# Attention with projected keys, then a gated feed-forward: an earlier projection, another tile for two sums, and two reorderings

## The chip, the cores and the metric

The kernel runs on one NeuronCore of one Trainium2 chip. The metric is the device time of one execution in microseconds. A core has five engines with an instruction queue each: TensorE (PE, matrix products into the eight PSUM banks), VectorE (DVE), ScalarE (ACT), GpSimd (POOL) and SyncE (SP). Each works its own queue in order and waits on semaphores for the others. Here GpSimd issues the loads from DRAM that also convert to bf16, and SyncE issues stores, transposing DMAs and small transfers. All DMAs run on the same 16 DMA engines.

## The reference

Inputs are q, k, v of shape (8 batches, 8 heads, 1024 positions, 64), the projections E and F (64 x 1024) and the weights w_in (512 x 2048) and w_out (2048 x 512), all float32.

```
k_proj = einsum('ks,bhsd->bhkd', E, k)
v_proj = einsum('ks,bhsd->bhkd', F, v)
attn   = softmax(q @ k_proj^T / 8)            # over the 64 projected positions
x      = attn @ v_proj, heads side by side    # (8192, 512)
h      = x @ w_in
g      = h / (1 + exp(-1.702 * h))
out    = g @ w_out                            # (8192, 512)
```

## The kernel before

**Tiling.** The 8192 tokens are cut into 16 blocks of 512 tokens; a batch is two blocks, so block j belongs to batch j // 2, and block 6 is the first of batch 3. For each batch the kernel loads k, v and q (`load`, `load_kv`, `load_q`), projects k and v over the sequence (`proj`: 32 matmuls into one PSUM bank), casts the projected k into `k_b`, transposes it by DMA into `kt`, casts the projected v into `vq`, and transposes q by DMA into `qT`. For each block it then computes the scores and their exponentials, the sums over the 64 projected positions, their reciprocals spread to all partitions by a trip through DRAM, the values times the reciprocals (giving `xT`), and the two products of the feed-forward.

**Feed-forward.** From block 1 (second product) and block 2 on, both products use a fast scheme: a two by two split of each product into seven products of sums instead of eight. The first product's seven are `P1` to `P7` of a unit `u0` to `u3`; they need the sums `xw` of x (`xs`, line 499) and the sums `late` of w_in. The second product's are `F1` to `F7`, each in two halves `.0` and `.1` of eight matmuls; they need the sums `sg` of g (`gs` and `g_sum`, line 507) and `tw` of w_out. The copies and additions between them are the `c`, `d` and `Fc`, `Fd`, `Fo` steps on VectorE and ScalarE. A next product adds onto a bank only once the copy of its earlier state is made.

**Order.** Blocks 0 and 1, and the first product of block 2, are issued by loops over slots: `at(j, slot, f)` puts `f` into block j's slot, and `filled` runs it there. Six sums of w_in (`w_in_sums`, lines 486 and 490) are put into slots 4, 6, 8, 10, 12 and 14 of block 2; the sums of g of that block follow slots 7, 13 and 15, ahead of what is in the slot. From then on, order is written out by hand: `STEPS` is a list of words for one block period, with a suffix such as `+1` for a step of the next block, and `AHEAD` is a list of steps of other blocks that are done at a given point of the first period, where there is no earlier period to have done them. `pj@6:7` in it means step `pj` for block 6 with its PSUM bank given as 7. A step's instructions go to the queues of several engines at once, so its place in the list is its place in each of these queues.

**Steps of the change.** `su` makes the sums of the exponentials of a block on TensorE (line 719), `den` copies them from PSUM to SBUF on VectorE (line 723), `ga` gathers them by DMA to a small tile (line 322), `rc` takes the reciprocals (line 727), `sr` writes them to DRAM (line 731) and `sb` spreads them into `rbc` by two DMAs (line 735). `mv` multiplies the values by `rbc` (line 713). `pj`, `kb`, `kd`, `vq` project a batch, cast and transpose (lines 183, 620, 748). `hold` copies one element of `kt` on GpSimd (line 740), so that what follows in GpSimd's queue waits until the transpose has landed. `ld` loads k and v of the next batch (line 58), `qd` transposes q (line 263) and then loads the next batch's q (line 70).

In the period from block 2 to block 3, the kernel before does `pj kb kd vq hold ld qd` of block 6 at the end, after `u0.g21` of block 3, and `rc sr sb` of block 4 after `F4.1` of block 2. The tile for `den` has one buffer:

```
            if j not in rdens:
                rdens[j] = att.tile([P, 2, TB], F32, name="den", bufs=1)
            nc.vector.tensor_copy(rdens[j][:, t, :], live[f"D{t}"])
```

In block 15, the last, the F words of `STEPS` run functions from `ffn2_parts`. A table `more` puts half 2.1 next to 7.0, so that the halves run as 1.0 1.1 2.0 6.0 6.1 2.1 7.0 5.0 5.1 7.1 4.0 4.1 3.0 3.1. There `7.1` is followed by an addition on VectorE (line 575), and 4.0 adds onto the bank that this addition reads.

Of the kernel before, what the change touches and what calls it, by code (L numbers as in the profile page):

```python
# [9 lines left out]
F32 = mybir.dt.float32  # L10
# [7 lines left out]
def kernel(ctx, tc, q, k, v, E, F,  # L18
# [5 lines left out]
    P = 128  # L24
# [5 lines left out]
    TB = 512  # L30
# [7 lines left out]
    att = ctx.enter_context(tc.tile_pool(name="att", bufs=2))  # L38
    work = ctx.enter_context(tc.tile_pool(name="work", bufs=2))
# [135 lines left out]
    kvps, qT, expT, xT, rbc, rdens = {}, {}, {}, {}, {}, {}  # L175
# [91 lines left out]
    def eight(outs, lhsTs, rhss, w=32):  # L267


        for i, ro in ((0, (LO, HI)), (1, (HI, LO))):  # L270
            for c in range(0, KP, w):
                for ri, r in zip((LO, HI), ro):
                    nc.tensor.matmul(outs[i][r.start + c:r.start + c + w], lhsTs[i][ri, c:c + w], rhss[i][ri],  # L273
                                     start=True, stop=True)
# [20 lines left out]
    def gelu_table():  # L295
        nc.scalar.preload_act_table(AF.Gelu_apprx_sigmoid)

    def x_of(h):
        if h not in xT:
            xT[h] = att.tile([P, KC, TB], BF16, name="xT")  # L300
        return xT[h]
# [192 lines left out]
    def x_sum(j, i):  # L494

        x = xT[j]
        x11, x12, x21, x22 = x[:, KLO, TLO], x[:, KLO, THI], x[:, KHI, TLO], x[:, KHI, THI]
        in0, in1 = ((x12, x11), (x22, xw[:, 0]), (x22, x12), (x21, xw[:, 1]))[i]
        nc.vector.tensor_tensor(xw[:, i], in0, in1, op=ALU.subtract)

    def g_sum(j, i, c0, n):

        lo, hi = slice(c0, c0 + n), slice(FH + c0, FH + c0 + n)
        g, t = gT, [sg[:, i, c0:c0 + n] for i in range(4)]
        in0, in1 = ((g[:, lo, THI], g[:, hi, THI]), (t[0], g[:, lo, TLO]), (g[:, lo, TLO], g[:, lo, THI]),
                    (g[:, hi, TLO], t[1]))[i - 1]
        nc.vector.tensor_tensor(t[i - 1], in0, in1, op=ALU.add if i == 1 else ALU.subtract)  # L507

    def ffn2_ops(j):
        g = gts[j]  # L510
        return {1: (g[:, FLO, TLO], b11), 2: (g[:, FHI, TLO], b21), 3: (sg[:, 3], b22),
                4: (g[:, FHI, THI], tw[:, 3]), 5: (sg[:, 0], tw[:, 0]), 6: (sg[:, 1], tw[:, 1]),
                7: (sg[:, 2], tw[:, 2])}
# [90 lines left out]
    def step(name, j, banks=None):  # L604
# [7 lines left out]
        i, t = p[0], int(p[-1]) if p[-1].isdigit() else p[-1]  # L612
        b, c = divmod(j, NB2)

        def new(n, shape):
            live[n] = bank(banks.pop(0) if banks else BANK[n], shape)
            return live[n]
# [12 lines left out]
        if i[0] == "F" and i[1:].isdigit():  # L630
            i = int(i[1:])
            n = ("FD", "FB", "FG")[OF[i]]
            if i in (1, 5) and t == 0:
                new(n, [P, 2, MH])
            x, w = ffn2_ops(j)[i]
# [21 lines left out]
        elif i[0] == "u":  # L657
            n, m = int(i[1]), int(i[1]) % 2
# [3 lines left out]
            u1, u2 = uu[0][:, m], uu[0][:, 2 + m]  # L662
            lo, hi = slice(2 * n, 2 * n + 2), slice(FH + 2 * n, FH + 2 * n + 2)
            if t[0] == "P":
                i = int(t[1])
                x = xT[j]
# [7 lines left out]
                for r in range(2):  # L674
                    for c in range(KC // 2):
                        f = (2 * n + r) * P
# [17 lines left out]
        elif i[:2] == "gs":  # L694
            g_sum(j, int(i[2]), 4 * t, 4)
        elif i == "xs":
            x_sum(j, t)
        elif i == "sc":
            if j not in expT:
                expT[j] = att.tile([P, HP, TB], BF16, name="expT", bufs=3)  # L700
            eight([new(f"S{t}{e}", [P, TB]) for e in range(2)], [kts[b % 2][:, 2 * t + e, :] for e in range(2)],
                  [qT[b][:, c * JB:(c + 1) * JB, 2 * t + e, :] for e in range(2)])
        elif i == "ex":
            u = int(p[1])
            nc.scalar.activation(expT[j][:, 2 * u + t, :], live[f"S{u}{t}"], AF.Exp, scale=scale)
        elif i == "gt":
            gelu_table()
        elif i == "va":
            eight([new(f"V{t}{e}", [P, TB]) for e in range(2)], [vqs[b % 2][:, 2 * t + e, :] for e in range(2)],
                  [expT[j][:, 2 * t + e, :] for e in range(2)])  # L710
        elif i == "mv":
            u = 2 * int(p[1]) + t
            nc.vector.tensor_tensor(x_of(j)[:, u, :], live[f"V{p[1]}{t}"], rbc[j][:, u, :], op=ALU.mult)  # L713
        elif i == "su":
            d_ps = [new(f"D{e}", [P, TB]) for e in range(2)]
            for q_ in range(HP):
                for e in range(2):
                    r = HI if (q_ + e) % 2 else LO
                    nc.tensor.matmul(d_ps[e][32 * q_:32 * q_ + 32], ones[r, :32], expT[j][r, q_, :], start=True, stop=True)
        elif i == "den":  # L720
            if j not in rdens:
                rdens[j] = att.tile([P, 2, TB], F32, name="den", bufs=1)
            nc.vector.tensor_copy(rdens[j][:, t, :], live[f"D{t}"])  # L723
        elif i == "ga":
            gather(j)()
        elif i == "rc":
            nc.vector.reciprocal(rdens[j], rdens[j])
        elif i == "sr":
            n = rdens[j].shape[1]
            rdr[j] = dram.tile([HP, 2, TB], F32, name="rdr")  # L730
            nc.sync.dma_start(out=rdr[j].rearrange("p e (r n) -> (p e r) n", n=n), in_=rdens.pop(j))
        elif i == "sb":
            rbc[j] = att.tile([P, HP, TB], F32, name="rbc", bufs=1)
            for e, r in enumerate((LO, HI)):
                nc.sync.dma_start(out=rbc[j][r], in_=rdr[j][None, :, e, :].to_broadcast([D, HP, TB]))
        elif i == "pj":
            kvps[b] = new("PJ", [P, H, D])
            proj(b)()
        elif i == "hold":
            nc.gpsimd.tensor_copy(held, kts[b % 2][:1, 0, :1])  # L740
        elif i == "ld" and b + 1 < B:
            load_kv(k, kt, b + 1, "k_sb")
            load_kv(v, vt, b + 1, "v_sb")
        elif i == "kb":
            tmps["kb"] = att.tile([KP, H, D], BF16, name="k_b")
            copy(tmps["kb"], kvps[b][LO])
        elif i == "kd":
            nc.sync.dma_start_transpose(out=kts[b % 2], in_=tmps["kb"].rearrange("k h d -> k (h d)"))
        elif i == "vq":
            r, xs_ = ((LO, X_LO), (HI, X_HI))[t]  # L750
            copy(vqs[b % 2][r].rearrange("k (u e) d -> k u e d", e=2),
                 kvps[b][HI].rearrange("k (u x) d -> k u x d", x=4)[:, :, xs_, :])
        elif i == "qd":
            q_dma(b)()
            if b + 1 < B:
                load_q(b + 1)
        elif i != "ld":
            raise KeyError(name)
# [14 lines left out]
    def at(j, slot, *fs):  # L773
        fill.setdefault((j, slot), []).extend(fs)
# [60 lines left out]
    at(2, 3, spread(3, nc.gpsimd), lambda: load(3))  # L835
    at(2, 1, proj(2), kv_out(2, nc.scalar.copy))
    for i, f in enumerate(w_in_sums()):
        at(2, 4 + 2 * i, f)
    def filled(j, slot):
        for f in fill.pop((j, slot), []):  # L840
            f()
# [2 lines left out]
    for j in range(NBLK):  # L844
# [9 lines left out]
        if j == 0:  # L854
            parts = [(n, range(8 * g, 8 * g + 8)) for n in range(JB) for g in range(2)]
# [10 lines left out]
        parts = ffn2_parts(j, 5, 6, 7, None)  # L866
        for s, (i, t) in enumerate((i, t) for i in (1, 5, 6, 2, 7, 4, 3) for t in range(2)):
# [4 lines left out]
        (2, None):  # L872
            "F1.0@2 F1.1@2 Fc1@2 sc.1@4 sc.0@4 ex.1.0@4 ex.1.1@4 F2.0@2 ex.0.0@4 ex.0.1@4 F2.1@2 sc.1@5 "
            "F6.0@2 sc.0@5 F6.1@2 ex.1.0@5 ex.1.1@5 ex.0.0@5 ex.0.1@5 gt@3 Fo0@2 Fc2@2 va.0@3:6,1 va.1@3:5,7 "
            "mv.0.0@3 mv.0.1@3 mv.1.0@3 mv.1.1@3 F7.0@2 su@4:0,3 den.0@4 den.1@4 ga@4 F7.1@2 ",
        (2, "F4.1"): "rc@4 sr@4 sb@4",
        (2, "u0.g21+1"): "pj@6:7 kb@6 kd@6 vq.0@6 vq.1@6 hold@6 ld@6 qd@6",
    }

    def ahead(j, after):  # L880
        for word in AHEAD.get((j, after), "").split():
            name, n = word.split("@")
            n, _, banks = n.partition(":")
            step(name, int(n), [int(x) for x in banks.split(",")] if banks else None)
            done.add((name, int(n)))

    done = set()
    for j in range(2, NBLK):
        last = j == NBLK - 1
        parts = ffn2_parts(j, BANK["FD"], BANK["FB"], 2, 5) if last else {}  # L890
        ahead(j, None)
        for word in STEPS:
            m = word.replace("-", "+-").split("+")
            name, n = m[0], j + int(m[1] if len(m) > 1 else 0)
            if last and name[0] in "Fs" and n == j and name[:2] not in ("sc", "su", "sr", "sb"):
                if name[1:2].isdigit() and name[0] == "F":
                    i, t = int(name[1]), int(name[3])
                    more = {(2, 1): [], (7, 0): [(2, 1), (7, 0)]}
                    for x in more.get((i, t), [(i, t)]):
                        parts.pop(x)()  # L900
            elif due(name, n, j) and (name, n) not in done:
                step(name, n)
            ahead(j, word)
# [33 lines left out]
```

## Time and profile before

| what | value |
|---|---|
| median of 5 runs | 491.95 us (489.44 to 492.51) |
| the profiled execution | 488.36 us |
| its span, first to last recorded work | 486.6 us |
| mean granted TensorE clock | 0.992 of full speed |
| TensorE matmuls busy | 467.2 us (96%) |
| VectorE busy | 316.7 us (65%) |
| ScalarE busy | 322.5 us (66%) |
| GpSimd busy | 83.8 us (17%) |
| read from and written to HBM | 72.88 and 16.99 MB |

Times inside a profile are microseconds from the start of its span. In the timeline, a line gives the start, the length, the engine with the line of the kernel, the operation, what it writes and reads, how many instructions are merged in it, and in brackets the idle time before it and what ended that. "PEld" is the loading of weights into TensorE and overlaps the matmuls; "SPq" is SyncE's issue of a DMA, whose data move later. In the table of waits a line is: who waited for whom, total us, number of waits, longest. The queue called q0 carries the DMAs that GpSimd issues, q1 those of SyncE and ScalarE; a share is that of 16 engines, and where packets of two transfers overlap in an engine the sum can exceed 100%.

### The profile page before, as it was taken

The numbers are of one execution on the slowest core, as the hardware profiler recorded it, in microseconds if no ns is written. First come the engines' busy times: TensorE is split into PE (matmuls) and PEld (weight loads), VectorE is DVE, ScalarE is ACT, GpSimd is POOL, SyncE is SP. The second block draws the span as 40 slices with busy tenths as digits, with TensorE's granted clock in tenths as the row PEclk, the third lists the DMA queues.
The fourth block names the chain that finished last, engine by engine and source line by source line (L and its number), as shares of the span: only waits on it lengthen the run. The fifth ranks groups of instructions, "written<-read, shape, count | busy, mean of one in ns | idle before, by whom it ended". The sixth has DMA issues, their size and how long they took to land.

```text
span 486.6 us, 10486 instructions
## 1 busy us (share of the span) xinstructions
PE 467.2 (96%) x4323; PEld 357.9 (74%) x4331; DVE 316.7 (65%) x587; ACT 322.5 (66%) x559; POOL 83.8 (17%) x104
## 2 busy tenths in 40 slices
PE   7999989998897999999999999999999999999996
PEld 3644447555676878787888878787888878888885
DVE  4503784587566576957768576957768585958561
ACT  2665463566376686967878686967878695758461
POOL 7562161061015010501014010500000000000000
PEclk9999998999899999999999999999999999999999
DMA  9999999989099999992999379982290413502022
GB/s 166 200 189 208 221 161 165 220 174 173 4 184 224 188 191 198 214 126 91 194 243 97 102 156 207 206 118 92 41 226 6 105 69 89 162 16 88 0 88 88
DMA packets 132963, 69.19 MB, mean 142 GB/s; under 512 B 98340, under 2 KB 122420, under 8 KB 132916
## 3 DMA queue, kind: packets, MB, share of 16 engines
q0 software_dynamic: 86816, 30.43, 56.5%
q1 hardware_dynamic: 46020, 37.84, 32.0%
q8 instruction: 34, 0.56, 0.5%
q10 hardware_dynamic: 80, 0.26, 0.3%
q14 instruction: 13, 0.11, 0.1%
HBM read 72.88 MB, written 16.99 MB: 185 GB/s over the span
## 4 chain that ended last, share of the span: by engine, by line
PE 75%; DMA 16%; DVE 4%; ACT 1%; issue 1%; POOL 1%; SPq 1%; DVEq 0%; POOLq 0%; ACTq 0%
PE k_ps L677 31%; PE k_ps L637 31%; PE k_ps L533 4%; DMA q_sb<-in_q_dram 4%; PE k_ps L273 3%; PE k_ps L183 2%; DMA w_in_sb<-in_moe_w_in_dram 2%; DMA w_out_sb<-in_moe_w_out_dram 2%; DMA v_sb<-in_v_dram 2%; DMA qT<-q_sb 2%; DMA kt<-k_b 2%; PE k_ps L426 1%; DVE sg L507 1%; DVE q_even L486 1%; ACT gT L693 1%
## 5 line engine op out<-in xcount | busy, mean ns | idle before, releaser
L623 DVE TENSOR_TENSOR q_even<-k_ps,q_even 128x512 f32<-128x512 f32 x104 | 70.5, 689 | 57.4 <-PE k_ps L677 55.7
L677 PE MATMUL k_ps<-xw,late 128*128 128x256 bf16 x624 | 89.6, 273 | 2.9 <-DVE den L723 2.2
L677 PEld LDWEIGHTS <-late 128*128 128x128 bf16 x832 | 80.5, 98 | 15.7 <-issue 3.0
L637 PEld LDWEIGHTS <-sg 128*128 128x128 bf16 x832 | 81.9, 99 | 12.9 <-issue 1.8
L637 PE MATMUL k_ps<-tw,sg 128*128 128x256 bf16 x624 | 78.6, 276 | 1.1 <-DVE sg L507 0.8
L693 ACT ACTIVATE gT<-k_ps 128x512 bf16<-128x512 f32 x104 | 62.2, 600 | 25.5 <-PE k_ps L677 24.0
L677 PEld LDWEIGHTS <-w_in_sb 128*128 128x128 bf16 x624 | 58.3, 98 | 16.7 <-issue 10.4
L620 ACT COPY q_even<-k_ps 128x512 f32<-128x512 f32 x65 | 37.0, 590 | 45.5 <-PE k_ps L677 45.4
L637 PEld LDWEIGHTS <-gT 128*128 128x128 bf16 x624 | 61.0, 98 | 7.8 <-issue 0.4
L677 PE MATMUL k_ps<-xT,w_in_sb 128*128 128x256 bf16 x416 | 62.2, 273 | 0.0
L693 ACT ACTIVATE gT<-q_even 128x512 bf16<-128x512 f32 x104 | 61.5, 632 | 0.0
L70 POOL DMA_DIRECT2D q_sb<-in_q_dram x48 | 42.7, 916 | 105.8 <-DMA qT<-q_sb 73.3
L637 PE MATMUL k_ps<-w_out_sb,gT 128*128 128x256 bf16 x416 | 51.6, 273 | 0.1
L507 DVE TENSOR_TENSOR sg<-gT 128x1024 bf16<-128x1024 bf16 (+2 forms) x64 | 41.4, 648 | 3.7 <-ACT gT L693 1.9
L426 PE MATMUL k_ps<-xT,w_in_sb 128*128 128x512 bf16 (+1 forms) x195 | 42.4, 370 | 0.3
L428 ACT ACTIVATE gT<-k_ps 128x512 bf16<-128x512 f32 (+1 forms) x50 | 28.9, 580 | 17.9 <-PE k_ps L426 17.7
L426 PEld LDWEIGHTS <-w_in_sb 128*128 128x128 bf16 x200 | 19.3, 98 | 21.3 <-issue 0.8
L713 DVE TENSOR_TENSOR xT<-k_ps,rbc 128x512 bf16<-128x512 f32 x52 | 33.5, 679 | 0.4 <-issue 0.4
L677 PE MATMUL k_ps<-xT,late 128*128 128x256 bf16 x208 | 31.2, 273 | 0.5 <-ACT q_even L620 0.5
L677 PE MATMUL k_ps<-xw,w_in_sb 128*128 128x256 bf16 x208 | 31.3, 273 | 0.0
L681 ACT COPY k_ps<-k_ps 128x512 f32<-128x512 f32 x52 | 29.1, 587 | 2.8 <-PE k_ps L677 2.0
L620 DVE COPY q_even<-k_ps 128x512 f32<-128x512 f32 x39 | 25.7, 686 | 8.1 <-PE k_ps L677 8.1
(135 smaller groups left out, 563.7 us busy)
## 6 DMA issues: line engine op xcount, KB each, us to landing
out_dram<-o_sb SPq DMA_DIRECT2D x31, 512.0 KB
rbc<-rdr SPq DMA_DIRECT2D x24, 512.0 KB
k_sb<-in_k_dram POOLq DMA_DIRECT2D x7, 1024.0 KB, 11.5
v_sb<-in_v_dram POOLq DMA_DIRECT2D x7, 1024.0 KB, 15.7
q_sb<-in_q_dram POOLq DMA_DIRECT2D x48, 128.0 KB, 6.5
w_in_sb<-in_moe_w_in_dram POOLq DMA_DIRECT2D x8, 256.0 KB, 11.1
w_out_sb<-in_moe_w_out_dram POOLq DMA_DIRECT2D x4, 512.0 KB, 11.5
q_even<-in_q_dram POOLq DMA_DIRECT2D x12, 128.0 KB, 14.6
```

The costliest lines, as they stand in the source:

```text
L70: nc.gpsimd.dma_start(out=qt[b][:, j], in_=qv[:, j])
L426: nc.tensor.matmul(h_ps, w_in_sb[:, kc, fc * P:(fc + 1) * P], xT[j][:, kc, ts], start=(kc == 0), stop=(kc == KC - 1))
L428: nc.scalar.activation(gts[j][:, fc, ts], h_ps, AF.Gelu_apprx_sigmoid)
L507: nc.vector.tensor_tensor(t[i - 1], in0, in1, op=ALU.add if i == 1 else ALU.subtract)
L533: nc.tensor.matmul(dst, a[:, k, tc_ * P:(tc_ + 1) * P], w[:, k], start=(first and (one or tc_ == 0) and k == 0), stop=(final and k == FH - 1),
L620: (nc.scalar.copy if n in ON_ACT else nc.vector.tensor_copy)(out_, in_)
L623: nc.vector.tensor_tensor(out_, in0, in1, op=ALU.add)
L637: nc.tensor.matmul(live[n][:, t], x[:, c, t * P:(t + 1) * P], w[:, c], start=(i in (1, 5) and t == 0 and c == 0), stop=(i in (2, 3, 4) and ...
L677: nc.tensor.matmul(live[h][:, r], a[:, c, f:f + P], w[:, c], start=(i in (1, 5) and r == 0 and c == 0), stop=(i in (2, 3, 4) and r == 1 an ...
L681: nc.scalar.copy(new(f"B{m}", [P, 2, TH]), live[f"A{m}"])
L693: nc.scalar.activation(out_, in_, AF.Gelu_apprx_sigmoid)
L713: nc.vector.tensor_tensor(x_of(j)[:, u, :], live[f"V{p[1]}{t}"], rbc[j][:, u, :], op=ALU.mult)
```

## The change

Four edits:

1. The sums of block 4 (`den`, only for block 4) go into the tile `o1_sb` of the pool `work`, which otherwise takes half of a block's output; the sums of all other blocks keep the tile `den`.
2. The last two of the six sums of w_in move from slots 12 and 14 of block 2 to slot 15, behind all sums of g of that block.
3. In the first hand-written period, half 7.1 of block 2's second product moves from the front to after `u1.c1` of block 3; the projection of batch 3 with its casts, its transpose `kd`, `hold` and `ld` moves forward to after `gs4.0` (which is `xs.3` of block 3 in the order of this period), and uses bank 1 in place of 7; `qd` moves to after `sb` of block 4.
4. In the last block the halves run as 1.0 1.1 2.0 6.0 6.1 5.0 5.1 7.0 7.1 2.1 4.0 4.1 3.0 3.1.

The number of instructions on each engine is the same.

```diff
         elif i == "den":
             if j not in rdens:
-                rdens[j] = att.tile([P, 2, TB], F32, name="den", bufs=1)
+                pool, n = (work, "o1_sb") if j == 4 else (att, "den")
+                rdens[j] = pool.tile([P, 2, TB], F32, name=n, bufs=1)
...
     for i, f in enumerate(w_in_sums()):
-        at(2, 4 + 2 * i, f)
+        at(2, (4, 6, 8, 10, 15, 15)[i], f)
...
-            "mv.0.0@3 mv.0.1@3 mv.1.0@3 mv.1.1@3 F7.0@2 su@4:0,3 den.0@4 den.1@4 ga@4 F7.1@2 ",
-        (2, "F4.1"): "rc@4 sr@4 sb@4",
-        (2, "u0.g21+1"): "pj@6:7 kb@6 kd@6 vq.0@6 vq.1@6 hold@6 ld@6 qd@6",
+            "mv.0.0@3 mv.0.1@3 mv.1.0@3 mv.1.1@3 F7.0@2 su@4:0,3 den.0@4 den.1@4 ga@4 ",
+        (2, "u1.c1+1"): "F7.1@2",
+        (2, "gs4.0"): "pj@6:1 kb@6 kd@6 vq.0@6 vq.1@6 hold@6 ld@6",
+        (2, "F4.1"): "rc@4 sr@4 sb@4 qd@6",
...
         parts = ffn2_parts(j, BANK["FD"], BANK["FB"], 2, 5) if last else {}
+        tail = [(1, 0), (1, 1), (2, 0), (6, 0), (6, 1), (5, 0), (5, 1), (7, 0), (7, 1), (2, 1), (4, 0), (4, 1)]
...
                 if name[1:2].isdigit() and name[0] == "F":
-                    i, t = int(name[1]), int(name[3])
-                    more = {(2, 1): [], (7, 0): [(2, 1), (7, 0)]}
-                    for x in more.get((i, t), [(i, t)]):
-                        parts.pop(x)()
+                    parts.pop(tail.pop(0))()
```

## The prediction

> **What bounds the kernel now.** I read the busy shares first (TensorE 96% of a 486.6 us span; the profiled execution took 488.36 us, so 1.76 lie around the span). Only TensorE's idle time can then be won, so next came its waits over the run:
>
> ```profile
> PE k_ps L273 <- DMA qT<-q_sb: 2.7, 1, 2.7
> ...
> PE k_ps L677 <- DVE den L723: 2.2, 1, 2.2
> ...
> PE k_ps L637 <- DVE sg L507: 0.8, 1, 0.8
> PE k_ps L533 <- DVE o_sb L575: 0.8, 1, 0.8
> ```
>
> Each happens once. The first three fall between 112 and 149 us, where blocks 2 and 3 meet; the fourth is in the last block. Between 180 and 460 us TensorE waits for nothing. The table by stretches (length, TensorE busy and matmuls, ..., granted clock, DMA share, GB/s) shows what the waits hide:
>
> ```profile
> 122.00:124.00 2.00, 0.09 (x1) 0.09 (x1) 1.43 (x3) 0.00 (x0) 0.00 (x0) 1.00 0.12 7
> 124.00:126.00 2.00, 2.00 (x12) 1.47 (x12) 1.39 (x3) 0.59 (x1) 0.00 (x0) 0.56 0.05 8
> 126.00:128.00 2.00, 2.00 (x13) 1.48 (x12) 0.00 (x0) 0.04 (x1) 0.00 (x0) 0.58 0.00 0
> 128.00:130.00 2.00, 2.00 (x21) 1.79 (x19) 1.53 (x3) 1.34 (x3) 0.00 (x0) 1.00 0.01 4
> ```
>
> After the wait on den the clock is near half for 4 us: 12 matmuls in 2 us, where 20 or 21 are normal. "Busy" conceals it. The DMA engines meanwhile stand still. Then the timeline of SyncE's and GpSimd's issues, batch 3's and the next batch's:
>
> ```profile
> 134.49 1.34 SPq L735 DMA_DIRECT2D rbc<-rdr  x2
> 137.10 1.23 SPq L748 DMA_TRANSPOSE kt<-k_b  x1
> 138.64 5.45 SPq L263 DMA_TRANSPOSE qT<-q_sb  x1
> ...
> 174.95 1.23 SPq L748 DMA_TRANSPOSE kt<-k_b  x1
> ...
> 184.71 1.26 SPq L735 DMA_DIRECT2D rbc<-rdr  x2
> 186.27 11.22 SPq L263 DMA_TRANSPOSE qT<-q_sb  x1
> ```
> ```profile
> 142.57 0.18 POOL L740 COPY held<-kt 1x1 bf16<-1x1 bf16 x1 [25.46 <-DMA kt<-k_b]
> 143.06 0.87 POOL L58 DMA_DIRECT2D k_sb<-in_k_dram  x1 [0.31 <-PE k_ps L677]
> ...
> 174.76 0.87 POOL L58 DMA_DIRECT2D k_sb<-in_k_dram  x1 [9.87 <-PE k_ps L677]
> ```
>
> Block 6's scores begin at 148.97, when qT has landed: **that landing, not the work before it, places everything after it.** What arrives at 146.3 or earlier waits. Last, the DMA queues (packets, MB, share) in 184 to 188 and then 188 to 192 us:
>
> ```profile
> q0 software_dynamic: 813, 0.83, 124.3%
> q1 hardware_dynamic: 5, 0.00, 0.2%
> ```
> ```profile
> q1 hardware_dynamic: 560, 0.87, 101.7%
> q0 software_dynamic: 54, 0.04, 6.5%
> ```
>
> While k and v load (q0), the rbc transfers issued at 184.71 (q1) move nothing until about 188, when the load is through; qT comes behind them and lands at 199.9, 13.6 us after its issue.
>
> **What the Trainium skill says.** "DMA: Bandwidth & Descriptors", section "Queues, rings and completion order": each DMA engine takes turns between queue rows by packets, not bytes. The trace agrees: loads of 1 KB packets run at 204 per us alone, and beside them kt's 256 B packets got 124 to 132 per us, the loads 157 to 162 (288 to 290 us). Alone, qT's packets run at 1133 per us. "TensorE: Matmul & The Clock Gate", part 1 on the HAM clock gate: an idle window of about 3.4 us halves the clock, and the window runs freely. The trace agrees in the size (0.56); 2.2 us of idle sufficed once, 2.7 us at 146 did not.
>
> **The change, part by part.** Times are the trace's, moved.
>
> *Two sums of w_in behind those of g.* VectorE's 2.29 us subtraction (106.76) and 1.22 us cast (110.97) go behind eight sums of g. F6.0's last matmul waited 0.84 for them; its successor at 112.98 comes at 111.97. No instruction is added, and late is first read at 118.9, after 113.1. **-1.0.**
>
> *Block 4's sums in o1.* den.0@5 waited 2.82 us for the gather of block 4 to read the one den tile. Now it follows the xw sums at 118.8, ends at 120.1, and u1.P5 goes at 120.64 for 123.91: **-3.3** with the first part. o1's earlier store was issued at 92.5, and its next writer, Fd1, comes 7 us after the gather: free. F7.1, moved behind block 5's sums, fills 0.87 us there; free. With the idle gone I take F5's 16 matmuls at full clock, 1.75 us for 3.50: **-4.9** at u1.P7 (127.76 becomes 122.8). If the clock is still halved, everything below is 1.75 later.
>
> *Projection of batch 3.* k and v landed by 116.2, so no data is awaited. But it takes bank 1, which u1.g11 still reads: in the trace that activation ends at 129.04, where the next matmul started at 128.20. So about 0.9 is a new wait; then 32 matmuls, 1.85 us, from 124.15 to 126.0. Behind it k_b is cast (+1.99 to +2.67 after its start), and vq.1 ends at +3.46; u3.P1 needs the same bank after 1.31 us of other matmuls: 0.35 more. Behind the cast on VectorE stand u1.d1 and Fd1, done by 128.2, before u1.P4 and F4.0 (128.1, 128.5) lose over 0.1. F4.1 comes at 129.85 for 131.69. At its old place 2.25 us fall away, so F3.0 is at 132.1 for 136.25: **-4.1**. That is all the compute gains before the scores of block 6.
>
> *Its DMAs.* kd goes at 126.85 (projection +2.70). DMA is idle, so it lands in some 2.1 us (issued at 339.18 in quiet, its packets ended at 341.1). The 1x1 copy "held" frees GpSimd at 129.0, and k and v of batch 4 are issued at about 129.5 for 143.06. rc, sr, sb follow u0.P7 as before: sr 131.1, sb 132.65 to 134.0, qd 134.1 for 138.64. **The order is turned over: the load goes ahead of rbc and qT.** A load issued at 174.76 kept the engines to 188.4, 13.6 us; this one to 143.1 alone. rbc is 1 MB at 112 packets of 2 KB per us, 4.4 us; qT's 4096 packets take 3.6. As the engines are full throughout, qT, last in its ring and of the smallest packets, ends at 129.5 + 13.6 + 4.4 + 3.6 = 151.1; with the 0.9 from last packet to landing seen at 199 us, **152.0 for 148.83: +3.1 at block 6's scores**. This price isn't in the trace of before: from below, qT keeps its 10.2 us (144.3); from above it adds the 3 us of gaps that its packets show between 192 and 199, or the late clock of F5: 155. I take the sum because it only assumes full engines.
> rbc itself lands at about 144 (shared by packets from 136 on), where mv.0.1@4 wants it at 138.2. On VectorE u2.d2 and u2.d1 are queued behind it, and u2.P4 waits for u2.d1: TensorE idles from 140.3 to about 146, then 2.0 us of work (144.3 to 146.3 in the trace; 3.7 at half clock) still reach the scores before 152. The wait is covered by qT's; without that cover it is 1.7 us over before. Such idling should halve the clock; part of the 1.75 us of one cold spell falls after 152: half, **+0.9**. Stores of block 2 wait behind qd on SyncE, until about 150; o0 is rewritten at 157: hidden, 1 us if not.
>
> *Last block.*
>
> ```profile
> 478.51 0.69 DVE L575 TENSOR_TENSOR o_sb<-k_ps,u_sb 128x512 f32<-128x512 f32 x1 [4.55 <-ACT u_sb L556]
> ...
> 479.25 1.91 PE L533 MATMUL k_ps<-tw,gT 128*128 128x256 bf16 x16 [0.84 <-DVE o_sb L575]
> ```
>
> With 2.1 (8 matmuls, 0.87 us) between 7.1 and 4.0, the 0.84 us wait is covered: **-0.85**. The store of o0's left half goes 3 us later, 0.26 MB ahead of the last ones; at 268 GB/s at most 1 us, hidden if it moves before 481.
>
> Sum: +3.1 + 0.9 - 0.85 = +3.1 us, 491.5 against 488.36. The median of the five runs is 3.6 above the profiled execution, so on its scale 491.95 + 3.1 = 495.0.
>
> **Rivals.**
> *Faster, qT lands early* (0.15). Where rbc and qT keep their trace durations under the load, qT lands at 144.3 and TensorE, at hand from 142.2, loses little: -4.6 - 0.85 = -5.4, 486.5. It decides from a landing before 147.4. For it: every compute wait named above does vanish, and at 149 to 153 us stores of 4 KB packets had over half the engines beside the load. Against: qT's packets are 256 B.
> *Stall only moved* (0.20). qT lands at 148 to 150; all compute gains end in a longer wait there and only the last block's remains: about -1, 491.
> *Two cold spells or late F5* (0.13). qT at 154 to 155 and a halved clock behind it: +5 to +6 and +1.75, 498 to 499.
> *The sum above* (0.52): landing 150 to 154, 493 to 497.
>
> **How the numbers follow.** The 8-in-10 range runs from 487.5 (within the first rival) to 499.5 (the third). The likeliest case's own is 493 to 497. 0.5% is 2.5 us, about what a measurement here can tell from no change. Faster: the first rival, 0.15. Same: the second and a sixth of the main case, 0.28. Slower: the rest, 0.57.
>
> **What would show it.** Right: no wait of F6.0 on sg, u1.P5 without idle, clock 1.00 in 118 to 124, one new wait of near 0.9 us at the projection, k_sb issued before the second rbc and qd, q1 near zero or sharing by packets for 10 us, TensorE idle ahead of u2.P4 on rbc and at block 6's scores on qT, landing near 152; no wait on L575. Wrong: qT landing under 147, or q0 starting behind qd.

## The result: 490.58 us, and the profile after

The changed kernel takes 490.58 us (median of 44 runs, 488.72 to 492.14), the kernel before 490.11 us (79 runs, 484.96 to 494.65). The medians differ by 0.5 us; the ratio is 1.002 with a 95% interval of 1.0008 to 1.0033, which is 0.4 to 1.6 us. So the changed kernel is slower, but by less than the 0.5% that the forecast calls measurable. The forecast was 495.0 us. The changed kernel's profiled execution took 491.15 us (span 489.3, mean clock 0.990), where the forecast on that scale was 491.5.

TensorE's waits after, whole run (who waited for whom, total us, number of waits, longest):

```profile
PE k_ps L637 <- DVE xT L713: 10.3, 1, 10.3
...
PE k_ps L533 <- ACT k_ps L564: 0.9, 1, 0.9
PE k_ps L183 <- ACT gT L693: 0.7, 1, 0.7
PE k_ps L677 <- DVE xw L499: 0.6, 1, 0.6
```

The waits on den, on sg, on qT and on the addition at line 575 are gone. In their place stand the new wait of the projection (line 183, 0.7 us) and one of 10.3 us on `mv` (line 713), which did not exist before. VectorE's line shows that `mv` itself waited for `rbc`, and the timelines of SyncE and GpSimd show why `rbc` was late:

```profile
147.76 0.69 DVE L713 TENSOR_TENSOR xT<-k_ps,rbc 128x512 bf16<-128x512 f32 x1 [11.43 <-DMA rbc<-rdr]
```
```profile
125.90 1.17 SPq L749 DMA_TRANSPOSE kt<-k_b  x1
130.13 0.34 SPq L732 DMA_DIRECT2D rdr<-rc  x1
136.63 1.34 SPq L736 DMA_DIRECT2D rbc<-rdr  x2
138.28 10.80 SPq L263 DMA_TRANSPOSE qT<-q_sb  x1
```
```profile
128.23 0.18 POOL L741 COPY held<-kt 1x1 bf16<-1x1 bf16 x1 [9.13 <-DMA kt<-k_b]
128.72 0.87 POOL L58 DMA_DIRECT2D k_sb<-in_k_dram  x1 [0.31 <-issue]
...
152.09 7.00 POOL L70 DMA_DIRECT2D q_sb<-in_q_dram  x8 [21.63 <-DMA qT<-q_sb]
```

The load of k and v is issued at 128.72, 1.4 us ahead of the small write `rdr` at 130.13. The spreading `rbc` must wait until that write has landed, and is issued at 136.63, 6.5 us behind it. In the kernel before, the write had gone out with no load beside it, and `rbc` followed at 134.49, 1.55 us behind:

```profile
132.94 0.34 SPq L731 DMA_DIRECT2D rdr<-rc  x1
```

qT, in the same queue, comes behind both. The DMA queues (packets, MB, share) in 132 to 134 and then in 134 to 136 us:

```profile
q0 software_dynamic: 397, 0.41, 123.8%
```
```profile
q0 software_dynamic: 361, 0.37, 112.8%
q1 hardware_dynamic: 141, 0.02, 12.5%
```

In the first of these stretches the write, issued two to four us earlier, moves no packet at all. In the second its packets get through beside the load. What this does to TensorE, by stretches (length, TensorE busy and matmuls, weight loads, VectorE, ScalarE, GpSimd, granted clock, DMA share, GB/s):

```profile
124.00:126.00 2.00, 2.00 (x21) 1.27 (x17) 0.81 (x2) 0.09 (x1) 0.00 (x0) 1.00 0.08 5
...
140.00:142.00 2.00, 0.00 (x0) 0.00 (x0) 0.00 (x0) 0.00 (x0) 0.00 (x0) 0.84 1.18 252
...
146.00:148.00 2.00, 0.00 (x0) 0.00 (x0) 0.24 (x1) 0.00 (x0) 0.00 (x0) 0.50 1.22 154
148.00:150.00 2.00, 1.49 (x8) 1.03 (x8) 2.00 (x4) 0.92 (x2) 0.00 (x0) 0.50 1.28 290
150.00:152.00 2.00, 2.00 (x13) 1.47 (x12) 2.00 (x5) 1.31 (x3) 0.00 (x0) 0.60 1.13 387
152.00:154.00 2.00, 2.00 (x31) 1.26 (x29) 2.00 (x5) 1.61 (x2) 1.91 (x3) 1.00 0.64 239
```

At 124 to 126 us, where the kernel before ran at half clock, 21 matmuls now pass in 2 us. From 138.2 to 148.5 TensorE stands still; then `rbc` has landed and the work that waited on it runs at half clock until 152. Block 6's scores follow without a wait of their own:

```profile
148.51 1.86 PE L637 MATMUL k_ps<-w_out_sb,gT 128*128 128x256 bf16 x8 [10.27 <-DVE xT L713]
...
152.70 0.63 PE L273 MATMUL k_ps<-qT,kt 64*32 64x512 bf16 x16
```

For comparing executions, I cut each into three by marks on TensorE: the end of the loading head (the start of the second group of matmuls of line 426 between 86 and 97 us), block 6's scores, and the first matmul of line 533 in the last block.

| execution | head | head to scores | scores to last block | last block to end | span | mean clock |
|---|---|---|---|---|---|---|
| before, profiled first | 93.55 | 55.42 | 319.07 | 18.56 | 486.6 | 0.992 |
| after, profiled first | 92.68 | 60.02 | 319.07 | 17.53 | 489.3 | 0.990 |

The change costs 4.60 us between head and scores and returns 1.03 in the last block. The head's 0.87 belongs to no edit: nothing in that part is changed. Heads of the same kernel differ by more than that: before_2 and before_3 below have 92.98 and 90.35.

### The profile page after: what moved, and what is told of

It reads as the page before. It is cut to its first block, busy times and chain, and to the rows that moved or that the text cites. A ratio compares the mean times of both kernels' runs of the same rounds, so it can differ in the third digit from the quotient of the medians.

```text
span 489.3 us, 10489 instructions
## 1 busy us (share of the span) xinstructions
PE 465.8 (95%) x4323; PEld 357.0 (73%) x4331; DVE 316.4 (65%) x587; ACT 322.2 (66%) x559; POOL 83.2 (17%) x104
## 4 chain that ended last, share of the span: by engine, by line
PE 73%; DMA 17%; DVE 5%; SPq 2%; ACT 2%; POOL 1%; issue 1%; DVEq 0%; POOLq 0%; ACTq 0%
PE k_ps L677 31%; PE k_ps L637 31%; PE k_ps L533 4%; DMA q_sb<-in_q_dram 4%; PE k_ps L273 3%; DMA v_sb<-in_v_dram 2%; DMA w_out_sb<-in_moe_w_out_dram 2%; DMA w_in_sb<-in_moe_w_in_dram 2%; DMA rbc<-rdr 2%; PE k_ps L183 2%; DMA kt<-k_b 2%; DMA rdr<-rc 1%; SPq L263 1%; DVE sg L507 1%; ACT gT L693 1%; DVE q_even L486 1%
## 5 line engine op out<-in xcount | busy, mean ns | idle before, releaser
L637 PE MATMUL k_ps<-tw,sg 128*128 128x256 bf16 x624 | 76.8, 273 | 0.3 <-DVE u_sb L620 0.3
L637 PE MATMUL k_ps<-w_out_sb,gT 128*128 128x256 bf16 x416 | 52.7, 276 | 10.4 <-DVE xT L713 10.3
```

The costliest lines, as they stand in the source:

```text
L637: nc.tensor.matmul(live[n][:, t], x[:, c, t * P:(t + 1) * P], w[:, c], start=(i in (1, 5) and t == 0 and c == 0), stop=(i in (2, 3, 4) and ...
```

## The experiments

I ask two things: why the stretch to the scores got longer although TensorE's old waits are gone, and why the median moved by some 0.5 us where the pair of profiles moved by 2.7 in the span. **Theory 1** for the first: the load of k and v ahead of `sr`, `sb` and `qd` makes `rbc` and qT late, and this takes back what the other edits gain. Each expectation names the other theories by what they foresee for that run. All times below are medians of at least six runs beside runs of the kernel before, except before_2, before_3 and after_2, which are one run each. A gain given in us is the ratio's share of the kernel before; the difference of the two medians is up to 1.2 us off it. The stretches between marks are from one execution each.

**load_last: the load of k and v put behind qT, all else as after.**

```diff
-        (2, "gs4.0"): "pj@6:1 kb@6 kd@6 vq.0@6 vq.1@6 hold@6 ld@6",
+        (2, "gs4.0"): "pj@6:1 kb@6 kd@6 vq.0@6 vq.1@6",
...
             q_dma(b)()
+            if j == 6:
+                nc.gpsimd.tensor_copy(held, qT[b][:1, 0, 0, :1])
+                load_kv(k, kt, b + 1, "k_sb")
+                load_kv(v, vt, b + 1, "v_sb")
```

> The changed kernel, but GpSimd's one-element copy that holds back the loads of batch 4's k and v reads qT of batch 3 in place of kt, so k and v are issued only when qT has landed. Theory 1 (the load was put ahead of rbc and qT on the DMA engines): rdr lands in 1.6 us again, rbc by about 138, no wait of TensorE ahead of u2.P4, qT by 142, block 6's scores at 141 to 143 where they were at 152.7; 8 to 11 us off the changed kernel, 480 to 482 us. Theory 2 (the wait belongs to the values and sums of block 4 themselves, and the load only happens beside it): mv of block 4 still waits near 10 us, 490 us.

Measured: 483.65 us (481.58 to 484.38), ratio 0.9855, 0.9817 to 0.9892; head to scores 51.84 us instead of 60.02, clock 1.00. Its SyncE timeline, and the wait that was left:

```profile
128.68 0.34 SPq L732 DMA_DIRECT2D rdr<-rc  x1
131.65 1.34 SPq L736 DMA_DIRECT2D rbc<-rdr  x2
133.31 7.31 SPq L263 DMA_TRANSPOSE qT<-q_sb  x1
```
```profile
PE k_ps L637 <- DVE xT L713: 3.3, 1, 3.3
```

Only the load of k and v moved, and the wait falls from 10.3 to 3.3 us: theory 1 holds, and theory 2, which foresaw an unchanged wait, falls. The time is some 2 us above what I expected: from `sr` to `sb` it still takes 3.0 us, with no load in the queues, and TensorE still waits for `rbc`.

**no_move: all edits but that of batch 3's steps.**

```diff
-        (2, "gs4.0"): "pj@6:1 kb@6 kd@6 vq.0@6 vq.1@6 hold@6 ld@6",
-        (2, "F4.1"): "rc@4 sr@4 sb@4 qd@6",
+        (2, "F4.1"): "rc@4 sr@4 sb@4",
+        (2, "u0.g21+1"): "pj@6:7 kb@6 kd@6 vq.0@6 vq.1@6 hold@6 ld@6 qd@6",
```

> The changed kernel with batch 3's projection, casts, transposes and loads back at the end of the period, bank 7; the other three edits and the place of F7.1 stay. Theory 1: all of it moves with TensorE, so the 4.9 us of compute gain and the 0.85 us of the last block get through: 5 to 7 us below before, 483 to 485 us, scores of block 6 at about 144. Theory 3 (the qT transfer has a landing time of its own that the compute gain can't move): only the last block's 0.85 us, 489 us.

Measured: 482.54 us (479.96 to 487.23), ratio 0.9824, 0.9781 to 0.9868; head to scores 50.48 us. Theory 3, which left only the last block's gain, falls. One wait is left there:

```profile
PE k_ps L273 <- DMA qT<-q_sb: 2.8, 1, 2.8
```

So the other edits together are worth 1.8%, some 8.6 us. Moving batch 3's steps lengthens the stretch from 50.48 to 60.02 and takes all of it back.

**move_only: the kernel before with batch 3's move alone**, the last diff the other way round, on the kernel before.

> The kernel before with only batch 3's steps moved to after gs4.0 and qd to after sb. Theory 1: the loads go out at about 134.5, the write of the reciprocals at about 136 stands behind them, and block 6's scores come 5 to 9 us later than 149: 495 to 499 us. Theory 3: 490 to 491 us.

Measured: 498.23 us (495.37 to 498.8), ratio 1.0147, 1.0108 to 1.0187; head to scores 67.64 us (the scores begin at 158.97, 10 us later than in the kernel before, a little past the range expected).

```profile
PE k_ps L637 <- DVE xT L713: 10.1, 1, 10.1
PE k_ps L677 <- DVE den L723: 4.3, 1, 4.3
```
```profile
135.85 0.34 SPq L731 DMA_DIRECT2D rdr<-rc  x1
142.47 1.33 SPq L735 DMA_DIRECT2D rbc<-rdr  x2
```

The wait of 10 us comes with the move alone, whatever the other edits do. The two experiments answer each other: some 8.6 us gained without the move, 7.2 lost with nothing else, and little left when both are made.

**o1_only: the kernel before with block 4's sums in the output tile and F7.1 behind `u1.c1`**

```diff
-                rdens[j] = att.tile([P, 2, TB], F32, name="den", bufs=1)
+                pool, n = (work, "o1_sb") if j == 4 else (att, "den")
+                rdens[j] = pool.tile([P, 2, TB], F32, name=n, bufs=1)
...
-            "mv.0.0@3 mv.0.1@3 mv.1.0@3 mv.1.1@3 F7.0@2 su@4:0,3 den.0@4 den.1@4 ga@4 F7.1@2 ",
+            "mv.0.0@3 mv.0.1@3 mv.1.0@3 mv.1.1@3 F7.0@2 su@4:0,3 den.0@4 den.1@4 ga@4 ",
+        (2, "u1.c1+1"): "F7.1@2",
```

> The kernel before with the second edit alone: block 4's sums in the output tile and F7.1 behind u1.c1 (batch 3 as before). Theory 1 (the step of the prediction: the wait on den was TensorE's own, and what gains on it reaches the scores as the projection and its DMAs behind move with it): no wait on den, head to block 6's scores 51 to 52.5 us instead of 54.7 to 58.6, wait on qT still 2 to 3; time 485.5 to 487 us, ratio 0.990 to 0.995, and, as one of the two idle stretches that cool the clock is gone, a narrower spread than the 9 us of the kernel before. Rival (the saved wait comes back on qT): qT wait 5 to 6 us, head to scores as before, ratio 0.998 to 1.002.

Measured: 483.91 us (481.71 to 485.44), ratio 0.9884, 0.9840 to 0.9928; head to scores 51.05 us. The wait on den is gone, the one on qT is as long as ever:

```profile
PE k_ps L273 <- DMA qT<-q_sb: 2.3, 1, 2.3
```

Theory 1 holds, and the rival falls: what this edit gains moves the projection, its DMAs and qT's landing along. The gain, 5.7 us, is more than I expected. The spread of its six runs is 3.7 us, against 7.6 in nineteen of the kernel before; with so unequal numbers that is no proof of a narrower one. (This expectation and the next number the edits in the prediction's order: "the second" is block 4's sums, "the first" the sums of w_in.)

**sums_only: the kernel before with the sums of w_in behind those of g**

```diff
-        at(2, 4 + 2 * i, f)
+        at(2, (4, 6, 8, 10, 15, 15)[i], f)
```

> The kernel before with the first edit alone: the last two sums of w_in behind those of g. The prediction gave it 1.0 us, as far as what follows moves with it. Theory 1: the wait of 0.8 us on sg is gone and the gather of block 4, and with it the end of the wait on den, comes as much earlier; head to scores 0.8 to 1.0 us less than in an execution of before with the same clock (54.7 at full clock), ratio 0.997 to 0.999. Rival: the gather ends where it did and the wait on den grows by the 0.8 us (4.3 to 4.6 us); ratio 0.999 to 1.001, head to scores 54.7 or more.

Measured: 490.19 us (486.79 to 492.69), ratio 0.9998, 0.9970 to 1.0026; head to scores 58.21 us.

```profile
PE k_ps L677 <- DVE den L723: 4.4, 1, 4.4
PE k_ps L273 <- DMA qT<-q_sb: 3.2, 1, 3.2
```

The wait on sg is gone from the list, and the one on den is 4.4 us. The three executions of the kernel before show 2.2, 3.7 and 3.6 there. This is the rival: TensorE arrives earlier and waits longer. The gather of block 4 was even issued 1.0 us earlier, counted from the head, than in before_3 (24.21 and 25.22 us), but the copy that waits for it began only 0.1 us earlier (30.26 and 30.40): the loads of q were still running in its way (see the last section). By itself the edit is worth nothing that can be seen.

**tail_only: the kernel before with the last block's new order**

```diff
+        tail = [(1, 0), (1, 1), (2, 0), (6, 0), (6, 1), (5, 0), (5, 1), (7, 0), (7, 1), (2, 1), (4, 0), (4, 1)]
...
-                    i, t = int(name[1]), int(name[3])
-                    more = {(2, 1): [], (7, 0): [(2, 1), (7, 0)]}
-                    for x in more.get((i, t), [(i, t)]):
-                        parts.pop(x)()
+                    parts.pop(tail.pop(0))()
```

> The kernel before with only the last block's new order. All theories: the wait of 4.0 on the addition is gone, 0.8 to 0.9 us below before (ratio 0.998), and the stretch from 110 to 160 us is as before; it shows how much that stretch differs from one execution of the same code to the next.

Measured: 489.1 us (484.97 to 491.84, 22 runs), ratio 0.9988, 0.9959 to 1.0016. The time alone says nothing. The last block's part of the trace says it: 17.75 us instead of 18.56, and no wait on line 575.

**before_2 and before_3: the kernel before, profiled twice more.** No edit. These and after_2 are for the second question.

> The kernel before, unchanged, profiled a second time, to see what of its profile repeats. Theory A (its executions differ in how many stretches of its head run at half clock, and the first profile was a lucky one): if this execution is longer than 489 us, its mean granted clock is below 0.991 and the extra lies between the head's end and block 6's scores (59 to 57 us instead of 55.4) or as a second half-clock stretch in the head. Theory B (the stretches repeat and the difference of 1.7 us between the first profile and the median lies outside the span): clock stays at 0.992, the stretch at 55.4 and the span at 486.6.

> The kernel before, unchanged, profiled a third time; the same as for before_2: theory A, the span follows the mean clock, some 1.5 to 2 us longer for each 0.002 to 0.003 of clock lost, and the place where it is lost changes; theory B, the same stretches to within 0.5 us.

Measured: 492.59 us (span 490.8, clock 0.993) and 484.48 us (span 482.7, clock 1.000). The waits of the one, then of the other:

```profile
PE k_ps L273 <- DMA qT<-q_sb: 4.3, 1, 4.3
PE k_ps L677 <- DVE den L723: 3.7, 1, 3.7
```
```profile
PE k_ps L677 <- DVE den L723: 3.6, 1, 3.6
PE k_ps L273 <- DMA qT<-q_sb: 2.3, 1, 2.3
```

Their idle time on den is equal to 0.1 us. What follows it is not. By stretches, before_2 and then before_3, columns as above:

```profile
124.00:126.00 2.00, 1.19 (x7) 0.88 (x7) 2.00 (x5) 0.38 (x1) 0.00 (x0) 0.78 0.00 1
126.00:128.00 2.00, 2.00 (x12) 1.38 (x10) 0.29 (x1) 0.21 (x1) 0.00 (x0) 0.50 0.05 7
...
152.00:154.00 2.00, 2.00 (x19) 1.42 (x12) 0.00 (x0) 2.00 (x5) 1.69 (x2) 0.60 1.11 327
154.00:156.00 2.00, 2.00 (x12) 1.40 (x11) 0.00 (x0) 1.98 (x4) 2.00 (x4) 0.55 1.20 271
```
```profile
122.00:124.00 2.00, 1.90 (x18) 1.70 (x18) 1.57 (x4) 0.58 (x1) 0.00 (x0) 1.00 0.05 8
124.00:126.00 2.00, 2.00 (x21) 1.80 (x19) 1.02 (x2) 1.08 (x2) 0.00 (x0) 1.00 0.00 0
```

before_2 runs at half clock behind both waits, before_3 behind neither. Head to scores is 58.55 and 54.72 us, scores to last block 320.74 and 319.08. So B falls, and A holds in the main: the kernel before has executions 8 us apart. Of these, 5.5 us (3.8 up to the scores, 1.7 behind them) are clock and landing times in and just behind the stretch that the change rewrites; the other 2.6 lie in the head. One number of the expectation was off: before_2 is above 489 us with a clock of 0.993, not below 0.991, since it also waited 2.0 us longer for qT than before_3 and had the longer head.

> The changed kernel, unchanged, profiled a second time. Theory A: its wait on the broadcast (10.3 us) sets the time of block 6's scores whatever the clock does ahead of it, so head-to-scores is 60.0 within 0.5 us and the time within 488.7 to 492. Theory B: the same. If the stretch differs by more than 1 us from 60.0, the pair of profiles cannot be read to the us and neither theory holds.

Measured: 490.5 us (span 488.6, clock 0.990); the wait on `mv` is 10.2 us, head to scores 60.63 (0.1 beyond what I allowed), scores to last block 319.07, last block 17.49. This execution repeats the first.

**early_rbc: load_last, with `rc`, `sr`, `sb` and `qd` moved forward as well, right behind the projection's transpose.**

```diff
-        (2, "gs4.0"): "pj@6:1 kb@6 kd@6 vq.0@6 vq.1@6",
-        (2, "F4.1"): "rc@4 sr@4 sb@4 qd@6",
+        (2, "gs4.0"): "pj@6:1 kb@6 rc@4 kd@6 vq.0@6 vq.1@6 sr@4 sb@4 qd@6",
```

> Batch 3's normaliser (rc, sr, sb) goes back to where the kernel before has it, at gs4.0, while its projection stays early, and batch 4's k and v are loaded only after qT has landed, as in load_last. Theory 1 (the load of k and v, put ahead of the small DMAs, is what batch 3's chain waits for): sr is issued near 126.5 us on an idle queue and the broadcast lands by 132, so the 3.3 us that load_last still waited on the broadcast goes; block 6's scores start at 140 to 141 us, ratio to before 0.975 to 0.982, 478 to 481.5 us. Rival (the chain's length no longer bounds; what is saved ahead of the scores comes back as a wait on qT or on the bank): scores at 142.5 to 143.5 us, ratio 0.984 to 0.988, the same as load_last.

(The expectation says that the kernel before has `rc`, `sr`, `sb` at `gs4.0`, and calls them batch 3's. They are block 4's, and it has them at `F4.1`, later in the period; the edit is as the diff shows.) Measured: 478.28 us (476.89 to 478.7), ratio 0.9776, 0.9737 to 0.9814; head to scores 48.28 us, clock 0.999.

```profile
124.68 1.17 SPq L749 DMA_TRANSPOSE kt<-k_b  x1
125.94 0.53 SPq L732 DMA_DIRECT2D rdr<-rc  x1
127.63 1.34 SPq L736 DMA_DIRECT2D rbc<-rdr  x2
129.28 8.02 SPq L263 DMA_TRANSPOSE qT<-q_sb  x1
```
```profile
139.98 0.88 POOL L58 DMA_DIRECT2D k_sb<-in_k_dram  x1 [0.31 <-issue]
```

The small write goes out at 125.94, its reader 1.7 us later, qT at 129.28, and only then, at 139.98, the load. TensorE waits neither for `mv` nor for den nor for qT, and block 6's scores begin at 139.77. The 3.3 us that load_last still lost are gone (51.84 to 48.28), and the rival, a new wait on qT or on the bank, did not come. This version is faster than both kernels, by some 11 to 12 us.

## Why the prediction was wrong, and where it was right

**The mechanism.** Parts 1 and 2 together are exact: u1.P7 went from 127.76 to 121.89, which is 5.0 us after taking off the head's 0.87, where the forecast has 4.96, and F5's matmuls run at full clock. The new wait at the projection is 0.7 for 0.9. Its DMAs up to `sr` come within 0.1 us of the forecast once the head is taken off: transpose at 125.90 (125.98), `hold` at 128.23 (128.13), load at 128.72 (128.63), `sr` at 130.13 (130.23). The turned-over order is what costs, as the prediction says: load_last shows it by moving the load alone, and no_move and move_only show that the wait goes and comes with batch 3's steps.

**Part 1** was booked as 1.0 us of its own. It is that only together with part 2: in sums_only it ends in a longer wait on den, and beside part 2 it is 1.0 us at u1.P7 (30.20 us behind the head in o1_only, 29.18 in no_move), of which 0.6 reach the scores. These are single executions.

**"Its DMAs": one term mis-sized, and the wait put in the wrong place.** The prediction took 1.55 us from `sr` to `sb`, as it was in quiet; under the load it was 6.5. So `rbc` landed at 147.7 instead of 143.1 (again without the head's 0.87), and TensorE came back at 148.5 instead of 145.1. That was not seen: I counted the share of the load against the large transfers, and none for the 128 small packets that must land before these may start. (By its own figures, 1 MB in packets of 2 KB at 112 per us, `rbc` takes 4.6 us and not 4.4, which changes little.) qT still landed near where the sum said. GpSimd, which waits for it, goes on at 152.09. In the kernel before it goes on 0.78 us after TensorE, which waits for the same landing:

```profile
148.97 0.62 PE L273 MATMUL k_ps<-qT,kt 64*32 64x512 bf16 x16 [2.67 <-DMA qT<-q_sb]
149.75 5.26 POOL L70 DMA_DIRECT2D q_sb<-in_q_dram  x6 [4.95 <-DMA qT<-q_sb]
```

Less the same 0.78, qT landed near 151.3 after the change, an estimate; the sum gave 151.1 (152.0 without the head's 0.87). But qT no longer bound: the prediction expected TensorE to wait for it at block 6's scores, and there is no such wait. The work of 2.0 us that "still reaches the scores before 152" began only at 148.5, ran at half clock until 151.7, and ended at 152.70. Thus the scores are 4.6 us later and not 3.1. The half clock behind them, priced at 0.9, cost nothing: it was over before they began, and scores to last block is 319.07 in both. The two errors make +4.6 for +4.0.

**The last block**: 1.03 us in the pair, 0.8 in tail_only, for 0.85.

Sum from the head on: +4.60 - 1.03 = +3.6 for a forecast +3.1. On the scale of the profiles, 491.15 us for 491.5. That these lie so close is in part luck, since the head was 0.87 us shorter, which no edit did: in the first profile of before, TensorE ran at half clock from 73 to 77 us, inside the head, and after the change it did not.

**The step that failed is the last one of the sum: "The median of the five runs is 3.6 above the profiled execution, so on its scale 491.95 + 3.1 = 495.0."** It takes the 3.6 us for a constant that the changed kernel keeps. The changed kernel's median is 0.57 *below* its profiled execution. Of the 4.4 us between forecast and measured median, 3.6 are this term; the 0.57 and the 0.35 by which the sum missed on the profiles make up the rest. Two things were in these 3.6. First, 491.95 was the median of five; that of all 79 is 490.11, 1.84 lower. Second, the profiled execution was 1.75 us better than that median (17 of the 79 runs are faster), in a kernel whose executions differ. Each comes with its own mean clock. One half-clock window of about 3.4 us (below) takes 0.0035 off it, so the number of windows can be estimated from the clock. I sorted the 57 runs of the kernel before that stand beside the experiments, and the 44 of the changed kernel, by the nearest number:

| half-clock windows | before: runs | median us | after: runs | median us |
|---|---|---|---|---|
| none | 4 | 485.75 | 0 | |
| 1 | 11 | 487.83 | 0 | |
| 2 | 14 | 489.72 | 0 | |
| 3 | 22 | 490.77 | 27 | 490.21 |
| 4 | 6 | 493.49 | 17 | 491.41 |

The first profiled execution of before has two windows (the windows at 120 to 130, and another at 70 to 80), before_2 two, before_3 none. The changed kernel has three or four, and in its two profiled executions all three lie in and just behind the wait of 10 us, where most of the half clock passes while TensorE has nothing to do. By the medians of the table the kernel before is 1 to 3 us slower with each window, about half of its runs have three or more of them, and the change takes away the place of one (den) and covers another (qT) while it adds its own wait. Against a clean execution like before_3 the change costs 6 us; against the typical one, nothing that counts. That the other runs of the table behave as the few profiled ones is argued from their clocks, not shown by traces.

The rival "stall only moved" foresaw 491 us, near the measured median, but by another way (a landing of qT at 148 to 150, and a gain of 1 us), and is not what happened; that its number fits is chance. The first and the third did not happen either.

## What to carry to other kernels

Here a bulk load issued 1.4 us ahead of a small write, on which a broadcast waits, delayed the whole chain, not by its share of the bandwidth but by the start and landing of that write (6.5 us where it was 1.55); holding the load until the last dependent transfer had landed, and sending the write earlier, made the changed kernel some 12 us faster. Before a gain or loss that was worked out from one profile is moved to the median, compare that profile's mean clock with those of the other runs: idle places that may or may not halve the clock make the offset a property of the kernel before, not of both. And where edits come together, undo them one at a time: here one part cost as much as the others together were worth, 8.6 us.

## What the runs showed of the hardware

**The half clock comes in windows of 3.4 us, and the idle time within one window decides, not the length of the wait.** The shortfall of the clock over the stretches of 5 us adds up to 3.4 us at half clock behind den in the first profile of before, 3.4 twice in before_2, 3.4 in tail_only, 6.8 and 3.4 in sums_only, 10.3 in the changed kernel. Where an execution has two separate stretches, their starts are a whole number of 3.413 us apart: 51.20 us in before (15 windows), 27.31 in before_2 and 27.30 in sums_only (8), 23.9 in move_only (7). The Trainium skill, "TensorE: Matmul & The Clock Gate", part 1 on the HAM clock gate, has the clock halved after an idle window of about 3.4 us, and says that the window runs freely. The traces agree with the size and the free run, but not with a window that must be wholly idle. If the nine profiled executions that have such a stretch behind a wait of TensorE are cut into windows on the raster that it gives, 1213 windows are at full clock. The 1200 of them that were followed by full clock hold at most 1.96 us of idle TensorE each; the 13 that were followed by half clock hold at least 2.01. So about 2.0 us of idle in one window sufficed here. A wait that lies across the edge of two windows can be longer and cost nothing: in the kernel before, 2.2 us on den lay in one window and cooled the clock, 2.7 us on qT were cut into 1.9 and 0.8 and did not. So one execution can differ from the next by where the edges fall. The figures take the busy time of matmuls as the profile models it.

**A small transfer starts late under a load.** In quiet, from `sr` to `sb` is 1.55 us (before) or 1.7 (early_rbc). Under the load of k and v it was 6.5 us (after) and 6.6 (move_only). In after, the write's first packets are seen at 134.25, 4.1 us behind its issue, where in before they are seen within 0.8 to 1.1 us; some two us more pass until all are through beside the load. The gather of block 4, for which den waits, does the same beside the loads of q: its first packets come 2.2 us behind its issue in before, 3.7 in before_3, 4.2 in sums_only and 4.3 in after. So the wait on den in the kernel before goes with the same late start as the wait that the change made. The skill's page "DMA: Bandwidth & Descriptors", section "Queues, rings and completion order", has the engines take turns by packets. That fits the sharing once it has begun (from 134.5 to 135.25 us, 105 packets of the write pass beside 125 of the load), and doesn't explain the late start, whose cause was not tried and stays open. The 3.0 us of load_last are another thing: there the write's packets start within 0.8 to 1.1 us as in quiet, but the last nine of 144 follow a us later. Why was not tried either.
